# Partial outputs summed in DRAM by transfers, and seven row groups in three fp32r passes

## The chip, the cores and the metric

The kernel runs on one core of a Trainium2 chip. The metric is the device time of one execution in microseconds (us); lower is better. Engines are named as in the profile: PE is TensorE's matmuls, PEld its weight loads, DVE is VectorE, ACT is ScalarE, POOL is GpSimd and SP is SyncE. POOL and SP here issue transfers and do almost nothing else.

## The reference

Four batches of q, k and v, each 6080 rows by 256 channels in float32, go through an attention over channels, and its output through a feed-forward layer whose weights are given in float64:

```python
qn = q / (norm(q, axis=1) + 1e-6);  kn = k / (norm(k, axis=1) + 1e-6)
s = kn.transpose(0, 2, 1) @ qn / tau          # 256 x 256 per batch
a = softmax(s);  x = (v @ a).reshape(24320, 256)
h = x @ w_in                                   # 256 -> 2048
g = where(h > 0, h, exp(min(h, 0)) - 1)
out = g @ w_out                                # 2048 -> 256
```

The kernel multiplies `a` into `w_in` once per batch, so that each token needs only two products.

## The kernel before, in words

A float32 product is made in one of two ways. A plain fp32 matmul reads float32 operands as they are. The other way splits each operand into a rounded part `hi` (fp32r; ACT's cast) and a rest `lo` (DVE's subtraction), and adds three fp32r matmuls: hi·hi, hi·lo and lo·hi. Work whose operands are split by ACT and DVE while PE does something else takes the second way.

The span falls into three stages.

- **Start (0 to 58 us).** Batch 0's Gram matrix k^T q, its softmax, the product with the first part of `w_in`, and the first three of batch 1's row groups. A row group is 256 rows of q and k (two rows on each of 128 partitions), 512 KB.
- **First chunks (58 to 244 us).** Tokens are cut into 48 chunks of 496 or 512 columns. The first four (`M = 4`) run in 64 steps; `take(i)` writes one. A step makes `ph` (six matmuls, `h_item`) for one 128-row slice of the hidden layer, lets ACT and DVE turn it into `e` and split it into `g` (`elu`, `split_g`), and multiplies the `g` of three steps earlier (`LAG = 3`) into the output banks `po` (six matmuls, `out_item`). `w_in` and `w_out` arrive as float64 and are converted during these steps, so a chunk can't take all 16 slices at once: `pieces` deals the 64 steps out as 13 pieces of four or eight steps. At the end of a piece `store` empties the two `po` banks: the first piece of a chunk by an ACT copy into `half[c]` in SBUF, the later ones by a DVE addition onto `half[c]`; the last sum goes to DRAM.
- **All other chunks (244 us to the end).** Pairs of chunks with seven products for eight (`product` and `multiply_out`). A small planner with queues per engine sets their order.

In the first two stages the order on PE, DVE and ACT is the order of the code (`tc.manual_schedule`). `at(step, fn)` hangs extra work on a step, at its end: conversions of the weights (`convert`), `w_in_ready` (two matmul groups `pw`, `wp` written from them), and, for batch 1's first 12 row groups (`EARLY`), their Gram products and sums of squares. Of these 12, five (`KEPT`) are multiplied by step 0. The other seven hang at `y = 10 + 3x`: load at step y, multiply at y + 3 by `early_items` (`multiply`: four plain fp32 matmuls of 256 columns into the bank `pe`), squares at y + 4, sum of squares by a transfer at y + 5. `keep_early` copies `pe` away at step 35. DVE and ACT take their instructions strictly in the order written, as the traces show below.

Of the kernel before, what the change touches and what calls it, by code (L numbers as in the profile page):

```python
# [54 lines left out]
def channel_attention_then_elu_ffn(ctx: ExitStack, tc, q, k, vT, tau, w_in, w_out, outT):  # L55
# [8 lines left out]
    nc = tc.nc  # L64
    B, N, C = q.shape
# [14 lines left out]
    M = 4  # L80
    Q = FT // 4
    pieces = []
# [14 lines left out]
    work = ctx.enter_context(tc.tile_pool(name="work", bufs=2))  # L97
# [309 lines left out]
    def span(c):  # L407

        b, x = divmod(c, NB)
        return b, b * N + sum(sizes[:x]), sizes[x]  # L410
# [82 lines left out]
    def store(c, f, po):  # L493
        _, t0, n = span(c)
        ov = outT[:, t0 : t0 + n].rearrange("(k p) t -> p k t", p=P)
        if c < M:
            o = half[c]
        else:
            o = work.tile([P, DT, CH], F32, tag="o", bufs=1, name="o")
        for dt in range(DT):  # L500
            y, x = quarters(o[:, dt, 0:n]), quarters_of_turns(po[dt][:, 0:n])
            if c < M and (c, 0, f + 1) not in pieces:
                nc.vector.tensor_add(y, y, x)
            elif c == NCH - 1 and dt == DT - 1:

                m = n // 2
                nc.scalar.copy(y, x)
                nc.sync.dma_start(ov[:, dt, 0:m], o[:, dt, 0:m])
                nc.scalar.dma_start(ov[:, dt, m:n], o[:, dt, m:n])
                continue  # L510
            else:
                nc.scalar.copy(y, x)
            if f == FT - 1:
                nc.sync.dma_start(ov[:, dt], o[:, dt, 0:n])


    wf = {}
# [42 lines left out]
    def scratch(x, k):  # L560
        return scr[:, x * KT * CH : (x + 1) * KT * CH].rearrange("p (k n) -> p k n", k=k)

    half = {c: scratch(c, k=DT) for c in range(M)}
    sq1 = scratch(M - 1, k=2 * 2).rearrange("p (t r) c -> p t r c", t=2)

    acc = new_acc(0)
# [2 lines left out]
    state = {}  # L569

    def multiply(raw, r, gram, first, last):

        for ct in range(KT):
            nc.tensor.matmul(  # L574
                gram[ct], raw[:, 1, r, ct * P : ct * P + P], raw[:, 0, r, :], start=first[ct], stop=last[ct]
            )
# [4 lines left out]
    with tc.manual_schedule(engines={nc.sync.engine}):  # L581
# [82 lines left out]
        def early_items(n, count=[0]):  # L664
            for _ in range(n):
                x, r = divmod(count[0], 2)
                count[0] += 1
                multiply(raw1[x], r, gram1, [x == 0 and r == 0, False], [False, (x, r) == (EARLY - 1, 1)])

        spread(pn, dg)  # L670
        vraw[1] = load_v(1)
# [48 lines left out]
    def at(step, fn, free=False):  # L720
        (loose if free else side).setdefault(step, []).append(fn)
# [12 lines left out]
    at(0, lambda: early_items(2 * KEPT - 6), True)  # L734
    def keep_early():
        state["early"] = tiny.tile([P, KT, C], F32, tag="early", bufs=1, name="early")
        nc.scalar.copy(state["early"], pe)


    wis = {}  # L740
# [125 lines left out]
    def new_row():  # L866
        state.setdefault("rows", []).append(work.tile([P, 2, 2, C], F32, tag="raw", bufs=5, name="raw_1"))

    def square_row(raw, first):
        for t in range(2):  # L870
            nc.scalar.activation(state["sum"][:, t] if first else raw[:, t], raw[:, t], AF.Square)

    def add_row(raw):
        for t in range(2):
            nc.gpsimd.dma_start(state["sum"][:, t], raw[:, t], accum_op=ALU.add)
# [3 lines left out]
        state[1, "acc"] = state["sum"]  # L879
        nc.sync.dma_start(state["sum"], x)  # L880

    at(10, lambda: [new_row() for _ in range(2)])
    at(10, lambda: state.__setitem__("sum", work.tile([P, 2, 2, C], F32, tag="raw", bufs=5, name="sum")))
    at(48, move_sum)
    for x, g in enumerate((*range(KEPT, EARLY), *range(KEPT))):
        y = 10 + SPACING * x
        at(y, lambda x=x, g=g: fill_rows(state["rows"][x % 2], 1, g))
        if g >= KEPT:
            at(y + 3, lambda x=x, g=g: (raw1.append(state["rows"][x % 2]), early_items(2)), True)
        at(y + 4, lambda x=x: square_row(state["rows"][x % 2], x == 0))  # L890
        if x:
            at(y + 5 if y + 5 < 47 else max(y + 5, 49), lambda x=x: add_row(state["rows"][x % 2]))
        if g == EARLY - 1:
            at(y + 7, keep_early, True)

    def store_half():
        c = steps[-1][0]
        _, t0, n = span(c)
        nc.sync.dma_start(outT[:, t0 : t0 + n].rearrange("(k p) t -> p k t", p=P), half[c][:, :, 0:n])

    at(52, store_half)

    def load_first_w():
        state["src"] = work.tile([P, KT, CH], F32, tag="raw", bufs=5, name="wraw_0")
# [284 lines left out]
    def copy_out(c, dt):  # L1189
        _, t0, n = span(c)  # L1190
        if c < M:
            o, to = half[c][:, dt, 0:n], outT[dt * P : dt * P + P, t0 : t0 + n]
            nc.scalar.copy(quarters(o), quarters_of_turns(out_bank(c, dt)[:, 0:n]))
            task(POOL, 0.6, lambda: nc.gpsimd.dma_start(to, o, accum_op=ALU.add), when=(10, 14)[dt], level=0)
            return
        assert all(len(y) == 2 for y in operands.values())
        x = exacts[dt][:, (c - M) % 2 * CH : (c - M) % 2 * CH + CH]
        o, to = x[:, 0:n], outT[dt * P : dt * P + P, t0 : t0 + n]
        if c == NCH - 1 and dt == DT - 1:
            m = n // 2  # L1200
            y, z = o.rearrange("p (r t) -> p r t", r=2), out_bank(c, dt)[:, 0:n].rearrange("p (q r s) -> p r s q", r=2, s=2)
            y = y.rearrange("p r (s q) -> p r s q", s=2)
            nc.vector.tensor_copy(y[:, 0], z[:, 0])
            nc.scalar.copy(y[:, 1], z[:, 1])
# [539 lines left out]
```

## Time and profile before

| what | value |
|---|---|
| median of 3 runs | 2066.98 us (2065.93 to 2067.82) |
| span of the profiled execution | 2065.1 us (the page gives no other time of it) |
| PE busy | 2056.3 us, 9965 matmuls |
| DVE busy | 1592.6 us |
| ACT busy | 1431.0 us |
| granted TensorE clock | 1.000 |
| PE busy in the stage of the change, 64 to 246 us | 181.60 of 182.00 us |

The span is 1.9 us below the median of the runs; that much lies around the first and last instruction or is spread between runs. A matmul's row gives its duration with the pipeline's tail (378 ns for 512 columns); what it costs in a row of matmuls is the distance between two starts (0.216 us). The same holds for ACT and DVE, where a row overlaps its successor by about 0.09 us.

### The profile page before, as it was taken

The page shows a single profiled execution, that of the slowest core. Times are in us where ns is not written, and L with a number is a line of the kernel's source. Part 1 is how long each engine was busy: PE and PEld are TensorE (multiplying, and loading weights), DVE is VectorE, ACT ScalarE, POOL GpSimd, SP SyncE. Part 2 cuts the span into 40 slices and gives each one's busy share as a digit, 9 for nine tenths or more (in the row PEclk, how much of TensorE's full clock was granted, in tenths as well). Part 3 has the DMA queues.
Part 4 walks back from the last instruction along what each step waited for, and adds up shares of the span by engine and source line. Part 5 has one row for each costly group of instructions (what it writes and reads, how often), then busy time and mean ns, then how long its engine had stood idle before and what let it go on. Part 6 is the DMA issues. An engine that isn't in the chain of part 4 may idle for free.

```text
span 2065.1 us, 30149 instructions
## 1 busy us (share of the span) xinstructions
PE 2056.3 (100%) x9965; PEld 1824.2 (88%) x9965; DVE 1592.6 (77%) x2521; ACT 1431.0 (69%) x2423; POOL 624.8 (30%) x1083
## 2 busy tenths in 40 slices
PE   9999999999999999999999999999999999999999
PEld 8888888899888888889998888888998888888998
DVE  6978887877788777777788777777778877777775
ACT  6878767667666776776766767667776666666675
POOL 0011134442222444443223344443322222222221
PEclk9999999999999999999999999999999999999999
DMA  9457677895576989986457699897645643553533
GB/s 352 136 157 211 185 216 223 231 268 153 177 221 184 288 233 277 258 218 207 152 178 234 173 284 256 234 282 209 185 158 192 198 159 107 169 162 107 164 125 118
DMA packets 213195, 415.21 MB, mean 201 GB/s; under 512 B 23216, under 2 KB 68912, under 8 KB 210992
## 3 DMA queue, kind: packets, MB, share of 16 engines
q0 software_dynamic: 154448, 294.78, 50.6%
q1 hardware_dynamic: 58448, 118.39, 17.6%
q8 instruction: 78, 1.28, 0.3%
q14 instruction: 77, 0.63, 0.1%
q10 hardware_dynamic: 144, 0.13, 0.0%
HBM read 145.03 MB, written 30.15 MB: 85 GB/s over the span
## 4 chain that ended last, share of the span: by engine, by line
PE 97%; DVE 1%; ACT 1%; DMA 1%; issue 0%; SPq 0%; POOL 0%; DVEq 0%; POOLq 0%
PE bank_b L1164 16%; PE po L1176 14%; PE po L1175 14%; PE po L1174 14%; PE bank_e L1164 11%; PE bank_a L1164 11%; PE gram L225 4%; PE gram L574 2%; PE ph L446 1%; PE ph L448 1%; PE ph L447 1%; PE po L488 1%; PE po L490 1%; PE po L486 1%; PE pe L574 1%; PE pw L818 1%
## 5 line engine op out<-in xcount | busy, mean ns | idle before, releaser
L1176 PE MATMUL po<-g,wo 128*128 128x512 f32 (+1 forms) x1416 | 535.0, 378 | 0.0
L1175 PE MATMUL po<-t,wo 128*128 128x512 f32 (+1 forms) x968 | 366.1, 378 | 0.0
L1174 PE MATMUL po<-t,wo 128*128 128x512 f32 (+1 forms) x968 | 365.1, 377 | 0.0
L1638 DVE TENSOR_TENSOR bank_e<-bank_b,p 128x512 f32<-128x512 f32 (+1 forms) x176 | 122.0, 693 | 277.2 <-PE bank_b L1164 268.1
L1176 PEld LDWEIGHTS po<-g,wo 128*128 128x128 f32 x1416 | 267.6, 189 | 34.5
L1628 ACT COPY bank_b<-bank_a 128x512 f32<-128x512 f32 (+1 forms) x176 | 99.5, 565 | 269.9 <-PE bank_a L1164 262.4
L1242 ACT ACTIVATE other<-other 128x512 f32<-128x512 f32 (+1 forms) x396 | 248.0, 626 | 12.6
L1259 POOL DMA_DIRECT2D t<-other x242 | 128.7, 532 | 413.2 <-DVE other L1245 249.2
L1259 POOL DMA_DIRECT2D t<-held x242 | 128.8, 532 | 294.9 <-DVE held L1245 117.2
L1174 PEld LDWEIGHTS po<-t,wo 128*128 128x128 f32 x968 | 183.0, 189 | 23.4
L1175 PEld LDWEIGHTS po<-t,wo 128*128 128x128 f32 x968 | 183.1, 189 | 22.6
L1242 ACT ACTIVATE held<-held 128x512 f32<-128x512 f32 (+1 forms) x308 | 193.2, 627 | 9.8
L225 PE MATMUL gram<-qk 128*128 128x256 f32 x720 | 196.3, 273 | 0.0
L1164 PE MATMUL bank_b<-t,s 128*128 128x512 f32 (+1 forms) x576 | 188.9, 378 | 1.6 <-DVE p L1655 1.6
L1259 POOL DMA_DIRECT2D g<-other x154 | 82.0, 532 | 334.1 <-DVE other L1245 191.8
L1175 PE MATMUL po<-g,wo 128*128 128x512 f32 (+1 forms) x448 | 169.8, 379 | 0.0
L1174 PE MATMUL po<-g,wo 128*128 128x512 f32 (+1 forms) x448 | 169.1, 377 | 0.0
L1266 DVE TENSOR_TENSOR g<-held,t 128x512 fp32r<-128x512 f32 (+1 forms) x242 | 162.3, 678 | 4.5 <-DMA t<-held 4.2
L1266 DVE TENSOR_TENSOR g<-other,t 128x512 fp32r<-128x512 f32 (+1 forms) x242 | 162.7, 680 | 0.5 <-DMA t<-other 0.5
L1241 ACT ACTIVATE other<-bank_a 128x512 f32<-128x512 f32 (+1 forms) x132 | 78.1, 592 | 116.6 <-PE bank_a L1164 114.6
L1164 PE MATMUL bank_b<-g,s 128*128 128x512 f32 (+1 forms) x432 | 147.0, 377 | 0.0
L225 PEld LDWEIGHTS gram<-qk 128*128 128x128 f32 x720 | 137.7, 191 | 4.6
(288 smaller groups left out, 4912.5 us busy)
## 6 DMA issues: line engine op xcount, KB each, us to landing
t<-held POOLq DMA_DIRECT2D x154, 256.0 KB, 3.4
t<-other POOLq DMA_DIRECT2D x154, 256.0 KB, 2.6
acc<-raw POOLq DMA_DIRECT2D x118, 256.0 KB, 5.3
g<-other POOLq DMA_DIRECT2D x98, 256.0 KB, 2.3
t<-held POOLq DMA_DIRECT2D x88, 248.0 KB, 2.3
t<-other POOLq DMA_DIRECT2D x88, 248.0 KB, 2.2
raw<-in_q_dram SPq DMA_DIRECT2D x76, 256.0 KB, 3.7
raw<-in_k_dram SPq DMA_DIRECT2D x76, 256.0 KB, 4.2
```

What stands on the lines that cost most here:

```text
L225: yield nc.tensor.matmul(gram[:, ct, :], hl[:, x, 1, r, cs], in_turns(hl[:, y, 0, r, :]), start=(first and ct == 0 and r == 0 and k == 0), ...
L574: nc.tensor.matmul(gram[ct], raw[:, 1, r, ct * P : ct * P + P], raw[:, 0, r, :], start=first[ct], stop=last[ct])
L1164: nc.tensor.matmul(bank[:, 0:n], w[:, x], y, start=(begin and k == 0), stop=(k == 2), skip_group_check=True)
L1174: yield nc.tensor.matmul(o, wo[:, f, 0, ds], hi, start=begin, stop=False)
L1175: yield nc.tensor.matmul(o, wo[:, f, 1, ds], hi, start=False, stop=False)
L1176: yield nc.tensor.matmul(o, wo[:, f, 0, ds], lo, start=False, stop=end)
L1241: nc.scalar.activation(e, h, AF.Relu, scale=-1.0)
L1242: nc.scalar.activation(e, e, AF.Exp, scale=-1.0)
L1259: nc.gpsimd.dma_start(hi, e)
L1266: nc.vector.tensor_sub(lo, e, hi.bitcast(F32))
L1628: nc.scalar.copy(vb, va)
L1638: nc.vector.tensor_add(ve, vb, vp)
```

## The change

Two things are changed, both in the second stage.

1. `store` no longer adds on DVE. Every piece's two banks are copied by ACT into one of two buffers in turn; the first piece of a chunk is stored to DRAM by SP, the later ones are added onto DRAM by a POOL transfer (`accum_op=ALU.add`). The final copy from the last bank (`copy_out`) takes the next buffer in turn. `half` shrinks from four tiles to two.
2. The seven row groups that hang on the steps take three fp32r passes. They are loaded into the two scratch tiles that came free. ACT makes `early_hi` at step y + 2, DVE makes `early_lo` at step y + 3, and PE multiplies at step y + 4 (`split_items`: twelve fp32r matmuls of 256 columns instead of four fp32 ones). The five groups before them stay in fp32, but read q's columns in the order that the fp32r ones use.

```diff
     def store(c, f, po):
-        if c < M:
-            o = half[c]
+        state["stored"] = state.get("stored", 0) + 1
+        o = half[state["stored"] % 2]
+        for dt in range(DT):
+            nc.scalar.copy(quarters(o[:, dt, 0:n]), quarters_of_turns(po[dt][:, 0:n]))
+        if (c, 0, f + 1) in pieces:
+            nc.sync.dma_start(ov, o[:, :, 0:n])
         else:
-            o = work.tile([P, DT, CH], F32, tag="o", bufs=1, name="o")
-        for dt in range(DT):
-            y, x = quarters(o[:, dt, 0:n]), quarters_of_turns(po[dt][:, 0:n])
-            if c < M and (c, 0, f + 1) not in pieces:
-                nc.vector.tensor_add(y, y, x)
...
+            nc.gpsimd.dma_start(ov, o[:, :, 0:n], accum_op=ALU.add)
...
-    half = {c: scratch(c, k=DT) for c in range(M)}
+    half = [scratch(x, k=DT) for x in range(2)]
...
+        def split_items(g):
+            hl = state["split"]
+            for r in range(2):
+                for ct in range(KT):
+                    for x, y in ((0, 0), (0, 1), (1, 0)):
+                        nc.tensor.matmul(
+                            gram1[ct],
+                            hl[x][:, 1, r, ct * P : ct * P + P],
+                            in_turns(hl[y][:, 0, r, :]),
...
+    def early_hi(raw):
+        if "split" not in state:
+            state["split"] = split_rooms(F32R, ("early_hi", "early_lo"))
+        nc.scalar.copy(state["split"][0], raw)
+
+    def early_lo(raw):
+        hi, lo = state["split"]
+        nc.vector.tensor_sub(lo, raw, hi.bitcast(F32))
...
     for x, g in enumerate((*range(KEPT, EARLY), *range(KEPT))):
-        y = 10 + SPACING * x
-        at(y, lambda x=x, g=g: fill_rows(state["rows"][x % 2], 1, g))
+        y, raw = 10 + SPACING * x, early_rows[x % 2]
+        at(y, lambda raw=raw, g=g: fill_rows(raw, 1, g))
         if g >= KEPT:
-            at(y + 3, lambda x=x, g=g: (raw1.append(state["rows"][x % 2]), early_items(2)), True)
-        at(y + 4, lambda x=x: square_row(state["rows"][x % 2], x == 0))
+            at(y + 2, lambda raw=raw: early_hi(raw))
+            at(y + 3, lambda raw=raw: early_lo(raw))
+            at(y + 4, lambda g=g: split_items(g), True)
+        at(y + 4, lambda raw=raw, x=x: square_row(raw, x == 0))
...
-    at(52, store_half)
```

The order on the engines moves at the first of the seven groups like this (steps 13 and 14; `cv` is a piece of `w_out` under conversion, `wp` of the product of attention and `w_in`, `e<-e,ph` is the last operation of `elu`, `g<-e,g` the rest of `split_g`). DVE before, from step 13's `e` to step 14's:

```order
L459 SCALAR_TENSOR_TENSOR e<-e,ph 128x512
L115 TENSOR_TENSOR g<-e,g 128x512
L129 TENSOR_SCALAR cv<-cv 128x1024
L131 TENSOR_SCALAR cv<-cv 128x1024
L404 SCALAR_TENSOR_TENSOR wp_380<-pw,sums,wp_380 128x512
L459 SCALAR_TENSOR_TENSOR e<-e,ph 128x512
```

DVE now, the same stretch:

```order
L459 SCALAR_TENSOR_TENSOR e<-e,ph 128x512
L115 TENSOR_TENSOR g<-e,g 128x512
L129 TENSOR_SCALAR cv<-cv 128x1024
L131 TENSOR_SCALAR cv<-cv 128x1024
L404 SCALAR_TENSOR_TENSOR wp_380<-pw,sums,wp_380 128x512
L904 TENSOR_TENSOR early_lo<-scr,early_hi 128x1024
L459 SCALAR_TENSOR_TENSOR e<-e,ph 128x512
```

`early_lo` stands behind everything else that DVE does for step 13.

PE now, where step 14's output matmuls end and its `pw` begins; before, this place held no Gram matmuls (they stood one step earlier):

```order
L490 MATMUL po_1_731<-g,wo 128x512
L672 MATMUL pe<-early_hi 128x256
L672 MATMUL pe<-early_lo,early_hi 128x256
L672 MATMUL pe<-early_hi,early_lo 128x256
L672 MATMUL pe<-early_hi 128x256
L672 MATMUL pe<-early_lo,early_hi 128x256
```

The second matmul of a group already reads `early_lo`, and all of the following steps stand behind it on PE.

ACT now, at the end of step 12 (before, the `CAST` of `early_hi` isn't there):

```order
L114 CAST g<-e 128x512
L127 ACTIVATE cv<-wo_1_378 128x1024
L900 CAST early_hi<-scr 128x1024
L457 ACTIVATE e<-ph 128x512
L458 ACTIVATE e<-e 128x512
```

`early_hi` stands between step 12's conversion and step 13's first ACT operation.

More of the change, by code (lines that the diff above doesn't have):

```diff
@@ L495, in store @@
         ov = outT[:, t0 : t0 + n].rearrange("(k p) t -> p k t", p=P)
-        if c < M:
-            o = half[c]
-        else:
-            o = work.tile([P, DT, CH], F32, tag="o", bufs=1, name="o")
-        for dt in range(DT):
-            y, x = quarters(o[:, dt, 0:n]), quarters_of_turns(po[dt][:, 0:n])
-            if c < M and (c, 0, f + 1) not in pieces:
[L503 to L514, printed above, removed]
+        state["stored"] = state.get("stored", 0) + 1
[4 more added lines that the diff above has]
+            nc.sync.dma_start(ov, o[:, :, 0:n])
+        else:
+            nc.gpsimd.dma_start(ov, o[:, :, 0:n], accum_op=ALU.add)
     wf = {}
@@ L667, in early_items @@
                 count[0] += 1
-                multiply(raw1[x], r, gram1, [x == 0 and r == 0, False], [False, (x, r) == (EARLY - 1, 1)])
+                for ct in range(KT):
+                    nc.tensor.matmul(
+                        gram1[ct],
+                        raw1[x][:, 1, r, ct * P : ct * P + P],
+                        in_turns(raw1[x][:, 0, r, :]),
+                        start=(x == 0 and r == 0 and ct == 0),
+                        stop=False,
+                        skip_group_check=True,
+                    )
+        def split_items(g):
+            hl = state["split"]
+            for r in range(2):
+                for ct in range(KT):
+                    for x, y in ((0, 0), (0, 1), (1, 0)):
+                        nc.tensor.matmul(
+                            gram1[ct],
+                            hl[x][:, 1, r, ct * P : ct * P + P],
+                            in_turns(hl[y][:, 0, r, :]),
+                            start=False,
+                            stop=((g, r, ct, x) == (EARLY - 1, 1, KT - 1, 1)),
+                            skip_group_check=True,
+                        )
         spread(pn, dg)
@@ L736, in keep_early @@
         state["early"] = tiny.tile([P, KT, C], F32, tag="early", bufs=1, name="early")
-        nc.scalar.copy(state["early"], pe)
+        for ct in range(KT):
+            nc.scalar.copy(halves(state["early"][:, ct]), halves_of_turns(pe[:, ct]))
     wis = {}
@@ L880, in move_sum, with split_rooms @@
         nc.sync.dma_start(state["sum"], x)
-    at(10, lambda: [new_row() for _ in range(2)])
+    def split_rooms(dtype, names):
+        return [work.tile([P, 2, 2, C], dtype, tag="raw", bufs=5, name=name) for name in names]
+    def early_hi(raw):
[5 more added lines that the diff above has]
+        nc.vector.tensor_sub(lo, raw, hi.bitcast(F32))
+    early_rows = [scratch(x, k=2 * 2).rearrange("p (t r) c -> p t r c", t=2) for x in (2, 3)]
+    at(10 + SPACING * (EARLY - KEPT) + 3, lambda: [new_row() for _ in range(2)])
     at(10, lambda: state.__setitem__("sum", work.tile([P, 2, 2, C], F32, tag="raw", bufs=5, name="sum")))
@@ L885, in channel_attention_then_elu_ffn @@
     for x, g in enumerate((*range(KEPT, EARLY), *range(KEPT))):
-        y = 10 + SPACING * x
-        at(y, lambda x=x, g=g: fill_rows(state["rows"][x % 2], 1, g))
+        y, raw = 10 + SPACING * x, early_rows[x % 2]
+        at(y, lambda raw=raw, g=g: fill_rows(raw, 1, g))
         if g >= KEPT:
-            at(y + 3, lambda x=x, g=g: (raw1.append(state["rows"][x % 2]), early_items(2)), True)
-        at(y + 4, lambda x=x: square_row(state["rows"][x % 2], x == 0))
+            at(y + 2, lambda raw=raw: early_hi(raw))
+            at(y + 3, lambda raw=raw: early_lo(raw))
+            at(y + 4, lambda g=g: split_items(g), True)
+        at(y + 4, lambda raw=raw, x=x: square_row(raw, x == 0))
         if x:
-            at(y + 5 if y + 5 < 47 else max(y + 5, 49), lambda x=x: add_row(state["rows"][x % 2]))
+            at(y + 5 if y + 5 < 47 else max(y + 5, 49), lambda raw=raw: add_row(raw))
         if g == EARLY - 1:
             at(y + 7, keep_early, True)
[L896 to L899, printed above, removed]
-    at(52, store_half)
     def load_first_w():
@@ L1191, in copy_out @@
         if c < M:
-            o, to = half[c][:, dt, 0:n], outT[dt * P : dt * P + P, t0 : t0 + n]
+            o, to = half[(state["stored"] + 1) % 2][:, dt, 0:n], outT[dt * P : dt * P + P, t0 : t0 + n]
             nc.scalar.copy(quarters(o), quarters_of_turns(out_bank(c, dt)[:, 0:n]))
```

## The prediction

> **What bounds the kernel now.** I read the page first: the span, PE's share, and the chain that ended last. Then came the busy times of the stage that is changed, and what PE waits for in it.
>
> ```profile
> span 2065.1 us, 30149 instructions
> PE 2056.3 (100%) x9965; PEld 1824.2 (88%) x9965; DVE 1592.6 (77%) x2521; ACT 1431.0 (69%) x2423; POOL 624.8 (30%) x1083
> ...
> PE 97%; DVE 1%; ACT 1%; DMA 1%; issue 0%; SPq 0%; POOL 0%; DVEq 0%; POOLq 0%
> ...
> 64.00:246.00 182.00, 181.60 (x839) 157.91 (x837) 153.94 (x227) 148.32 (x256) 23.95 (x28) 1.00 0.57 159
> ...
> PE po L488 <- DVE wo L549: 0.2, 1, 0.2
> ```
>
> PE is the bound, and in the changed stage it is as good as full: 181.60 of 182.00 us, with one wait of 0.2 us. DVE (153.94) and ACT (148.32) are less full, but not by much. So two things count: the matmul time that is taken from PE, and every wait that is put in front of PE where none was. Work taken from DVE is worth nothing by itself, since PE does not wait for it here.
>
> **The change part by part.** *The matmuls.* These are PE's rows around the first of the seven groups (steps 13 and 14), and two neighbours of the fp32r Gram form from a later batch:
>
> ```profile
> 94.72 1.89 PE L574 MATMUL pe<-raw 128*128 128x256 f32 x8
> ...
> 97.74 0.38 PE L446 MATMUL ph<-scr_r,wp 128*128 128x512 f32 x1
> ...
> 98.82 0.38 PE L448 MATMUL ph<-scr_r,wp 128*128 128x512 f32 x1
> ...
> 100.11 0.38 PE L490 MATMUL po<-g,wo 128*128 128x512 f32 x1
> ...
> 317.12 0.27 PE L225 MATMUL gram<-qk 128*128 128x256 f32 x1
> 317.23 0.38 PE L1175 MATMUL po<-g,wo 128*128 128x512 f32 x1
> ```
>
> One group is four fp32 matmuls, shown as eight records; 1.89 less a tail of 0.16 (0.38 less the 0.216 between starts) is 1.73 us. Now it is twelve fp32r matmuls of 256 columns; such a matmul moves the next start by 0.11 us (317.12 to 317.23), so 1.32 us. That is 0.41 us less a group, **2.9 us less** for seven. Above 0.11 the price is bounded by 0.21, if a weight load (0.19 us in its row below) could not run under so short a matmul; I take 0.11, the form's own row. The five groups before stay fp32 at the same count; that they read their columns in another order I cost at nothing, within 0.2 us.
>
> *The wait that is added.* A group now needs `early_lo`, which DVE makes at the end of the step before. These are ACT's and DVE's rows there, and the means of the conversion pieces that stand ahead of it:
>
> ```profile
> 90.31 1.04 ACT L114 CAST wi<-wf 128x1024 fp32r<-128x1024 f32 x1
> 91.26 0.59 ACT L457 ACTIVATE e<-ph 128x512 f32<-128x512 f32 x1
> ...
> 94.39 0.58 ACT L457 ACTIVATE e<-ph 128x512 f32<-128x512 f32 x1
> 95.00 0.63 ACT L458 ACTIVATE e<-e 128x512 f32<-128x512 f32 x1
> ...
> 99.23 0.60 ACT L457 ACTIVATE e<-ph 128x512 f32<-128x512 f32 x1 [0.61 <-PE ph L448]
> ```
>
> ```profile
> 91.47 1.22 DVE L115 TENSOR_TENSOR wi<-wf,wi 128x1024 fp32r<-128x1024 f32 x1
> ...
> 95.66 0.69 DVE L459 SCALAR_TENSOR_TENSOR e<-e,ph 128x512 f32<-128x512 f32 x1 [1.77 <-ACT e L458]
> 96.27 0.68 DVE L115 TENSOR_TENSOR g<-e,g 128x512 fp32r<-128x512 f32 x1
> 96.87 0.69 DVE L129 TENSOR_SCALAR cv<-cv 128x1024 f32<-128x1024 f32 x1
> 97.59 0.69 DVE L131 TENSOR_SCALAR cv<-cv 128x1024 uint32<-128x1024 uint32 x1
> 98.66 0.75 DVE L404 SCALAR_TENSOR_TENSOR wp<-pw,sums,wp 128x512 fp32r<-128x512 f32 x1 [0.38 <-ACT wp L403]
> 100.53 0.69 DVE L459 SCALAR_TENSOR_TENSOR e<-e,ph 128x512 f32<-128x512 f32 x1 [1.11 <-ACT e L458]
> ```
>
> The first group by itself. `early_hi` is a 1024-wide cast, 0.95 us of ACT (90.31 to 91.26), put where ACT has no gap: step 13's first ACT operation moves from 94.39 to 95.34, and with it DVE's `e` from 95.66 to 96.61. Behind it follow, at the distances of the rows, `g` 97.22, L129 97.82, L131 98.54, L404 99.15 (0.61 on; `pw` now ends 1.73 earlier, so ACT no longer delays it), and `early_lo` 99.81. That is an operation like the L115 of 1.22 us, so it ends at 101.03. PE meanwhile: step 13's output matmuls end at 94.72; `pw` (six at 0.216) to 96.02; step 14's hidden and output matmuls 2.59 us (97.74 to 100.33) to 98.61; hi·hi to 98.72. Then it waits for `early_lo`: **2.4 us** with 0.05 for the signal.
>
> The other six by the same count. From the last hidden matmul (98.82) ACT begins 0.41 later (99.23), DVE's `e` 1.30 after that (100.53); `g` 0.60 and a gap of 0.60, then 1.22 for `early_lo`: 102.95. PE comes to the lo matmul at 100.33 + 2.59 + 0.11 = 103.03. So a step with nothing else has 0.08 us to spare, and what stands between `g` and `early_lo` becomes the wait. By the order these are L143 at step 16, L129 and L131 at 19, L141 at 22, nothing at 25, L133 at 28 and L141 at 31:
>
> ```profile
> L133 DVE SCALAR_TENSOR_TENSOR cv<-wo,cv 128x1024 uint32<-128x1024 uint32 x3 | 4.5, 1492 | 0.0
> L141 DVE SCALAR_TENSOR_TENSOR cv_s<-wi,cv_s 128x1024 f32<-128x1024 uint32 x3 | 4.5, 1487 | 0.0
> L141 DVE SCALAR_TENSOR_TENSOR cv_s<-wo,cv_s 128x1024 f32<-128x1024 uint32 x3 | 4.2, 1397 | 0.0
> L143 DVE TENSOR_TENSOR cv<-cv,cv_s 128x1024 f32<-128x1024 f32 x3 | 3.7, 1218 | 0.0
> ...
> L457 ACT ACTIVATE e<-ph 128x512 f32<-128x512 f32 x63 | 37.2, 591 | 26.9 <-PE ph L448 26.9
> ...
> 114.79 0.38 PE L448 MATMUL ph<-scr_r,wp 128*128 128x512 f32 x1
> ...
> 116.67 0.57 ACT L457 ACTIVATE e<-ph 128x512 f32<-128x512 f32 x1
> ```
>
> Less 0.09 of overlap each: 1.13 + 1.32 + 1.40 + 0 + 1.40 + 1.31 = 6.6, less six times 0.08 is 6.1 us. That is the lower end, with 0.6 for the first group if `early_hi` cost nothing there: 6.7 in all. The upper end lets `early_hi` push every step by its full 0.95 (5.7) and keeps 2.4 for the first: 14.2; lateness that ACT has anyway comes on top. I take the middle that the rows give. ACT waits for PE 26.9 us ahead of 63 such operations, 0.43 each, so `early_hi` pushes by 0.52: 6.1 + 3.1 + 2.4 = 11.6. At step 19 ACT is already late: 116.67 against 114.79 + 0.41, by 1.47 us; I count half of that, since the waits before let ACT catch up, and as much again for DVE's backlog and ACT's store copies, so 1.2: **12.8 us of waits**.
>
> A wait also costs PE a restart. The longest wait of before, in the third stage, shows it, with the clock's first matmuls of the span beside it:
>
> ```profile
> 268.30 0.38 PE L1176 MATMUL po<-g,wo 128*128 128x512 f32 x1
> 270.08 0.92 PE L1164 MATMUL bank_b<-t,s 128*128 128x512 f32 x3 [1.41 <-DVE p L1655]
> 270.83 0.38 PE L1174 MATMUL po<-g,wo 128*128 128x512 f32 x1
> ...
> 268.14 0.68 DVE L1266 TENSOR_TENSOR g<-other,g 128x512 fp32r<-128x512 f32 x1
> ...
> 3.80 2.05 PE L574 MATMUL gram<-ragged 128*128 128x256 f32 x4
> 6.50 1.91 PE L574 MATMUL gram<-room 128*128 128x256 f32 x8
> ```
>
> After the gap three matmuls take 0.75 us instead of 0.65: 0.1 a wait, **0.7 us** for seven. The same rows show that PE does not go past a matmul that waits: L1174, whose `g` DVE had finished by 268.82, starts at 270.83. Were PE able to pass it, the seven waits would cost little and the sum would be the 2.9 us of gain. The Trainium skill ("TensorE: Matmul & The Clock Gate", "Part 2: What happens when you issue a matmul") says that only weight loads are pulled ahead and that matmuls stay in program order; by that rule the waits count in full, and the trace agrees with the 270.83 above.
>
> *The stores.* DVE loses 16 additions, ACT gains 16 copies:
>
> ```profile
> L503 DVE TENSOR_TENSOR scr<-scr,po 128x512 f32<-128x512 f32 x16 | 10.3, 686 | 0.0
> L512 ACT COPY scr<-po 128x512 f32<-128x512 f32 x8 | 4.3, 582 | 0.0
> ...
> acc<-raw POOLq DMA_DIRECT2D x118, 256.0 KB, 5.3
> ...
> raw<-in_q_dram SPq DMA_DIRECT2D x76, 256.0 KB, 3.7
> ```
>
> 16 × 0.60 us off DVE and 16 × 0.49 onto ACT, with seven `early_hi` 14.5 us in all, against 182.00 − 148.32 = 33.7 us that ACT has free. PE gains nothing from DVE's freed time; it can lose where ACT is full for a while, 0 to 1 us, and I take 0. The eight transfers that add onto DRAM stand on POOL's queue behind ACT's copies. Their nearest row is the adding transfer of half the size, 5.3 us to landing; a buffer is used again two pieces later, at least eight steps of 2.59 us, so even 10.6 us are hidden. On that queue `s<-x` for the third stage's second quarter now stands behind the last three of them, while DVE's work just ahead of that stage gets shorter. What that does to the stage's first waits I bound by the 1.41 us of the longest, gained or lost once more, and take 0. SP's queue gets four small stores earlier and loses later ones. The loads (3.7 us) have two steps, 5.2 us, before `early_hi`; late ones would stop ACT, which the range has to carry.
>
> **Sum.** −2.9 + 12.8 + 0.7 = +10.6 us on the profiled span of 2065.1, so 2075.7. The median of the runs lies 1.9 us above that span: **2077.6 us**.
>
> **The rivals.**
> - *The gain arrives.* DVE and ACT run so far ahead that `early_lo` is there: 2067.0 − 2.9 = 2064.1 us. For it: DVE is idle a sixth of the stage. Against it: both engines begin a step's work only when its hidden matmuls end, so free time before that cannot be used; it decides where the chain above is shorter than PE's 4.2 us from 98.82 to 103.03. With the third stage's wait of 1.41 us gone too, it would be 2062.7.
> - *The short matmuls cost 0.21.* Twelve weight loads in a row do not hide: 7 × 12 × 0.1 = 8.4 us more, 2086. Against it: in the row at 317.23 the next load hid under one short matmul; for it: there the neighbours are long.
> - *The clock.* At the span's start a record of the same fp32 matmul costs 0.51 us (2.05 for four), later 0.24 (1.91 for eight). If each of the seven waits brought that back for as long as it lasted at the start, at most to 5.85 us (3.80 + 2.05), half of that would be lost: 2.9 us each, 20 in all, 2098. Against it: the gap of 1.77 us before 270.08 was followed by near full rate. The Trainium skill (same page, "Part 1: The HAM clock gate") gives 3.4 us of idling as the window after which the clock halves; the waits above stay under it, so by that rule this does not happen.
>
> **How the numbers follow.** Waits as worked out: 0.73, with its own range from 2065.1 + 1.9 − 2.9 + 6.7 + 0.7 − 1.5 = 2070 to 2083 (14.2 and 2.4 more for lateness and late loads, with 1.5 of the seam, the 1.41 rounded). The gain arrives: 0.12 at 2064, and 0.04 at 2062.7 with the later wait gone. Short matmuls dear: 0.07. Clock: 0.04. The range 2069 to 2087 leaves out the second and the last, 0.2. A measurement of this kernel tells about 0.2%, 4.1 us: slower by more is the first case nearly whole with the last two, 0.82; faster by more only the one at 2062.7, 0.04; the rest 0.14.
>
> **What would show it.** Seven PE waits on DVE's `early_lo` between 95 and 175 us, 1 to 3 us each, at the second matmul of a group; PE busy lower by about 3 us and idle higher by about 13; no PE wait on the stores; the third stage the same as before but 10 us later. The prediction is wrong if these waits are absent or short, if ACT stops at `early_hi` for a load, or if a group's twelve matmuls take more than 1.4 us of PE without a wait.

## The result and the profile after

The changed kernel takes 2083.18 us in the median of 5 runs (2082.73 to 2083.79), against 2066.98 us for the kernel before in the same comparison: a ratio of 1.0081 (95% interval 1.0070 to 1.0091), so it is slower by 0.8%. The profiled execution took 2083.44 us, with a span of 2081.7 us.

The page of the changed kernel, the same parts that were shown of before:

```profile
span 2081.7 us, 30227 instructions
PE 2060.9 (99%) x9993; PEld 1825.8 (88%) x9993; DVE 1592.6 (77%) x2512; ACT 1444.9 (69%) x2447; POOL 635.3 (31%) x1091
...
PE 91%; ACT 3%; DVE 3%; issue 2%; DMA 1%; POOL 0%; ACTq 0%; POOLq 0%; DVEq 0%
```

The span grew by 16.6 us. PE was to become less busy and became busier, by 4.6 us. The chain that ended last was PE for 97% and is PE for 91% now: ACT and DVE have come into it, which means that PE stands and waits for them. The 4.6 us of busy time are, within 0.1, half rate and turned reads, which are read below, and the restart and the tail of a matmul at each of seven waits, less what the shorter matmuls save.

What PE waits for (total us, times, longest), whole span of the changed kernel:

```profile
PE pe L672 <- DVE early_lo L904: 12.1, 7, 2.6
PE bank_b L1184 <- DVE p L1675: 1.6, 2, 1.4
```

These are the seven waits of the forecast, at the line of `split_items`, and this list has no other new one in the stage. The wait at the third stage's beginning is as before. Weight loads have a list of their own (PEld), and it has two new waits at steps 44 to 46, small ones; the experiment e8 comes back to them:

```profile
PEld po L490 <- DVE g L115: 0.5, 1, 0.5
PEld po L486 <- ACT g L114: 0.3, 1, 0.3
```

The stage by windows of 15 us (length, PE busy and its matmuls, granted clock, DMA share, GB/s):

```profile
90.00:105.00 15.00, 12.66 (x60) 0.91 0.35 141
105.00:120.00 15.00, 12.96 (x65) 0.97 0.37 113
120.00:135.00 15.00, 12.38 (x56) 0.89 0.52 112
```

PE idles for 2.0 to 2.6 us in each of them. The clock column shows something that the kernel before did not have in this stage, where it was 1.00 throughout: 0.91, 0.97 and 0.89 around the first and the third group.

### The profile page after: what moved, and what is told of

Same layout as the page of the kernel before. It is cut to its first block, busy times and chain, and to the rows that moved or that the text cites. A ratio compares the mean times of both kernels' runs of the same rounds, so it can differ in the third digit from the quotient of the medians.

```text
span 2081.7 us, 30227 instructions
## 1 busy us (share of the span) xinstructions
PE 2060.9 (99%) x9993; PEld 1825.8 (88%) x9993; DVE 1592.6 (77%) x2512; ACT 1444.9 (69%) x2447; POOL 635.3 (31%) x1091
## 3 DMA queue, kind: packets, MB, share of 16 engines
q0 software_dynamic: 156624, 298.98, 51.5%
## 4 chain that ended last, share of the span: by engine, by line
PE 91%; ACT 3%; DVE 3%; issue 2%; DMA 1%; POOL 0%; ACTq 0%; POOLq 0%; DVEq 0%
PE bank_b L1184 16%; PE po L1195 14%; PE po L1196 14%; PE po L1194 14%; PE bank_e L1184 11%; PE bank_a L1184 11%; PE gram L225 4%; PE gram L563 2%; ACT e L457 1%; PE pe L658 1%; PE pe L672 1%; PE pw L830 0%; PE pw L829 0%; PE pw L828 0%; DVE g L115 0%
```

## The waits and the clock, row by row

PE's rows of the changed kernel at the first three groups (start, duration; in brackets the idle time before and what released it):

```profile
100.03 0.27 PE L672 MATMUL pe<-early_hi 128*128 128x256 f32 x1
102.64 0.58 PE L672 MATMUL pe<-early_lo,early_hi 128*128 128x256 f32 x1 [2.34 <-DVE early_lo L904]
103.01 0.42 PE L672 MATMUL pe<-early_hi,early_lo 128*128 128x256 f32 x1
...
104.93 0.42 PE L672 MATMUL pe<-early_hi,early_lo 128*128 128x256 f32 x1
105.14 0.63 PE L396 MATMUL pw<-wi,aT_split 128*128 128x512 f32 x1
105.57 0.53 PE L397 MATMUL pw<-wi,aT_split 128*128 128x512 f32 x1
105.94 0.38 PE L398 MATMUL pw<-wi,aT_split 128*128 128x512 f32 x1
...
114.57 0.27 PE L672 MATMUL pe<-early_hi 128*128 128x256 f32 x1
116.88 0.38 PE L672 MATMUL pe<-early_lo,early_hi 128*128 128x256 f32 x1 [2.04 <-DVE early_lo L904]
117.09 0.28 PE L672 MATMUL pe<-early_hi,early_lo 128*128 128x256 f32 x1
117.20 0.28 PE L672 MATMUL pe<-early_hi 128*128 128x256 f32 x1
...
125.98 0.27 PE L672 MATMUL pe<-early_hi 128*128 128x256 f32 x1
128.88 0.38 PE L672 MATMUL pe<-early_lo,early_hi 128*128 128x256 f32 x1 [2.62 <-DVE early_lo L904]
...
129.76 0.42 PE L672 MATMUL pe<-early_hi,early_lo 128*128 128x256 f32 x1
...
130.61 0.63 PE L446 MATMUL ph<-scr_r,wp 128*128 128x512 f32 x1
...
133.17 0.38 PE L486 MATMUL po<-g,wo 128*128 128x512 f32 x1
```

Read the distance between starts. The second group is as forecast: one wait, then 0.11 us from matmul to matmul. After the first wait the distance is 0.21 until 104.93 and 0.43 for the `pw` behind, so everything takes twice its time; from 105.94 on it is normal. After the third wait PE works at full rate for 0.9 us, and only from 129.76 on, in the middle of the group, at half rate, until 133.17. That second stretch is 3.41 us long, and none of its matmuls waits for anything.

DVE's rows at the third group show what PE waits for: `early_lo` stands behind both conversion pieces and ends at 128.82, and PE goes on at 128.88.

```profile
126.28 0.69 DVE L129 TENSOR_SCALAR wf<-wf 128x1024 f32<-128x1024 f32 x1
127.00 0.69 DVE L131 TENSOR_SCALAR wf<-wf 128x1024 uint32<-128x1024 uint32 x1
127.60 1.22 DVE L904 TENSOR_TENSOR early_lo<-scr,early_hi 128x1024 fp32r<-128x1024 f32 x1
```

From the seven pairs of rows (first matmul to second, less the 0.11 that it would take) the waits sum to 2.50 + 2.20 + 2.79 + 1.40 + 0.94 + 1.55 + 1.85 = 13.2 us. The second matmul then takes 0.21 (116.88 to 117.09), so a restart is 0.1, in seven groups another 0.8: 14.0 us. The matmuls themselves are twelve at 0.11, 1.33 us a group, so 2.8 us less than the 7 × 1.73 of before. Half rate costs 1.57 us within the first and third group, 0.37 in the `pw` behind the first and 1.26 in the six `ph` behind the third: 3.2 us.

One more term shows before the stage. PE's rows of the five groups that stayed fp32, at 49 us, in the changed kernel:

```profile
48.97 3.44 PE L658 MATMUL pe<-scr 128*128 128x256 f32 x12
52.24 0.49 PE L357 MATMUL pt<-ident,a 128*128 128x128 f32 x3
```

and the same twelve in the kernel before:

```profile
49.47 2.75 PE L574 MATMUL pe<-scr 128*128 128x256 f32 x12
52.06 0.67 PE L357 MATMUL pt<-ident,a 128*128 128x128 f32 x3
```

Twelve records took 2.59 us and take 3.27 now: 0.273 apiece for 0.216. Only the order in which they read q's columns was changed. For the forty records of five groups that is 2.2 us, by the starts of all their rows.

The sum is 14.0 − 2.8 + 3.2 + 2.2 = 16.6 us. The rows above stand 0.5 us earlier than those of before at this point, so the steps should start 16.1 us later behind the groups; from step 48 on they start 16.05 us later. That this agrees so closely is partly luck: up to step 10 the steps have lost 1.9 us and not 2.2, and steps 35 to 48 add 0.2 that is not in the sum (0.5 less at step 35, where a pause of before is gone, and 0.7 more at the two waits of the weight loads). The last 0.5 us to the 16.6 of the span come after that.

## The experiments

The theory at that point: PE loses by the waits for `early_lo`, by half rate after the longer ones, and by the turned reads of the fp32 groups; the stores cost nothing. The rival: the stores, with eight more transfers on POOL's queue, carry part of the loss by themselves.

**e1, the stores alone.** All twelve groups are multiplied in fp32 at y + 3, in plain column order, as before.

```diff
-            at(y + 2, lambda raw=raw: early_hi(raw))
-            at(y + 3, lambda raw=raw: early_lo(raw))
-            at(y + 4, lambda g=g: split_items(g), True)
+            at(y + 3, lambda raw=raw: (raw1.append(raw), early_items(2)), True)
...
-                        in_turns(raw1[x][:, 0, r, :]),
+                        raw1[x][:, 0, r, :],
```

> Only the stores by transfer; the seven row groups stay four plain fp32 matmuls at step y + 3, straight from the scratch tiles, and the five earlier groups read in plain order. Theory: the stores cost and bring nothing, since PE waited for no store before and ACT and POOL have the room: 2066.0 to 2068.5 us, no PE wait above 0.5 us between 64 and 246 us. Rival: the additions in DRAM or ACT's copies cost part of the 16 us: 2070 us or more, with PE waits on ACT or on g in that stage.

Measured: 2074.29 us in the median, ratio 1.0033 (1.0021 to 1.0046), and widely spread: 2068.97 to 2077.37 in six runs, where the kernel before stays within 3.7 us in 33. The expectation missed that. The profiled execution was the fastest of the six and shows no wait in the stage longer than 0.2 us, so it could not say what the others lost; e11 below does.

**e2, one more step for `early_lo`.** The changed kernel with the multiplications at y + 5.

```diff
-            at(y + 4, lambda g=g: split_items(g), True)
+            at(y + 5, lambda g=g: split_items(g), True)
```

> The changed kernel with split_items one step later (y + 5 instead of y + 4), nothing else. Theory: the 13.2 us of waits on early_lo and the 3.2 us of slow clock behind them vanish: 2083.2 - 16.4 = 2066.8 us (2065.5 to 2069), clock 1.000, no PE wait on early_lo. Rival: the wait only changes its place, since early_hi of the next group now needs the tile that PE still reads: ACT stops there and PE waits for g, 2072 us or more.

Measured: 2076.71 us (2073.32 to 2078.55), ratio 1.0046 (1.0034 to 1.0058). The waits for `early_lo` are gone as expected (0.2 us is left), but a gain of 16 was expected and 6.5 came. PE's and ACT's longest waits in the stage, then SP's:

```profile
PE ph L446 <- DVE e L459: 5.3, 1, 5.3
ACT early_hi L900 <- DMA scr<-in_k_dram: 6.5, 1, 6.5
```

```profile
SPq L159 <- DMA sum<-scr: 74.5, 18, 11.9
```

At one place ACT stood 6.5 us at `early_hi` for raw rows that had not landed, DVE's `e` came late behind it, and PE stood 5.3 us. SP must not write the tile before the transfer that adds up its squares has read it (L159 waits for `sum<-scr`, up to 11.9 us). That wait is as long in the kernel before, so it is not new by itself:

```profile
SPq L159 <- DMA sum<-raw: 74.2, 16, 13.0
```

New is that ACT, and behind it PE, stand when such a load comes later than usual. So a second wait stands behind the first one, in the loads; e11 shows what makes one late.

**e3, the waits filled.** The changed kernel with matmuls of a zero weight (256 columns, 4 to 18 a group) put where PE waits, so that the waits stay and PE does not stand idle.

```diff
+                        for _ in range(fill):
+                            nc.tensor.matmul(
+                                gram1[ct], zeros, in_turns(hl[0][:, 0, r, :]), start=False, stop=False, skip_group_check=True
+                            )
```

> The changed kernel, with 16, 14, 18, 8, 4, 9 and 12 matmuls of zero weights put behind the first matmul of the seven groups, so that PE works through most of each wait (0.11 us each) and idles 1.2 us at most. Theory: the waits stay (PE still needs early_lo at the same time) and the clock no longer falls: 2083.2 - 3.2 = 2080.0 us (2079 to 2081), clock 1.000, all L672-type matmuls 0.11 us apart. Rival: the slow matmuls behind the waits are not from idling: 2083 us or more with the 0.21 us distances still there.

Measured: 2080.4 us (2079.69 to 2081.01), as expected, 2.8 us below the changed kernel, although the changed kernel has fewer matmuls to do. The first and third of the windows above, and the wait that is left:

```profile
90.00:105.00 15.00, 14.45 (x81) 1.00 0.35 141
120.00:135.00 15.00, 14.38 (x82) 1.00 0.44 107
```

```profile
PE pe L678 <- DVE early_lo L915: 3.3, 7, 0.6
```

The clock is 1.00 in both, and over the whole span. Half rate after the waits is a cost of its own, of about 3 us, and it comes from PE standing idle, not from the twelve short matmuls.

**e4, plain column order.** The changed kernel, with q's columns read in plain order by both kinds of groups.

```diff
-                        in_turns(raw1[x][:, 0, r, :]),
+                        raw1[x][:, 0, r, :],
...
-                            in_turns(hl[y][:, 0, r, :]),
+                            hl[y][:, 0, r, :],
```

> The changed kernel with all reads of q's columns for the bank pe in plain order, the five fp32 groups and the seven fp32r ones, and the copy of pe in plain order. Theory: the five groups' records go back from 0.27 to 0.216 us apart, 2.3 us less, and the fp32r matmuls keep 0.11: 2080.9 us (2080 to 2082). Rival: an fp32r matmul needs the turned order for its rate and takes 0.2 us in plain order: seven groups 7.5 us longer, 2088 us.

Measured: 2080.66 us (2079.87 to 2082.04), 2.5 us below the changed kernel, with 11.8 us of waits for `early_lo`. The twelve fp32 records are back at 2.59 us:

```profile
48.70 2.75 PE L658 MATMUL pe<-scr 128*128 128x256 f32 x12
51.29 0.77 PE L357 MATMUL pt<-ident,a 128*128 128x128 f32 x4
```

These rows, and not the time, show the price of the turned reads. The time met its expectation, but it holds other terms too: this profile has one stretch at half rate (126.7 to 130.1 us) where the changed kernel has two, about 1.5 us less, and its fp32r matmuls take 0.119 us apiece for 0.111, which is 0.7 more.

**e5, e2 without the sums.** As e2, but the transfers that add up batch 1's squares are not issued (their sums are left out beyond the first group).

> As the kernel with the split multiplications one step later (2076.7 us), but without the eleven transfers that add up batch 1's squares (their sums are left out beyond the first group). Theory: what was left of its loss is late loads: a load waits for the summing transfer of the group before to have read its scratch tile, ACT stops at `early_hi` for the load, and PE for ACT's `e` (5.3 us at one place of its profile). Without the transfers the loads start in time, no PE wait on `e` or `early_lo` above 0.5 us is left in the stage, and the time is 2066.8 us (2065.5 to 2068.5): 2066.3, less 2.9 for the fp32r matmuls, plus 2.3 for the five fp32 groups' turned reads and about 1 for a restart or two. Rival: the loss comes from ACT's copies or the DRAM additions themselves: the time stays at 2073 or above.

Measured: 2066.77 us (2065.71 to 2067.90), ratio 1.0001 (0.9992 to 1.0009). The forecast was 2066.8. No PE wait is left in the stage, and ACT no longer waits for a load. So what e2 still lost goes with the sums. Leaving them out takes away their transfers as well as the wait of the loads for them; the rows of e2 and e11 are what names the loads.

**e6, `early_lo` first.** The changed kernel with `early_lo` ahead of the step's conversion on DVE, the multiplications still at y + 4.

```diff
-            at(y + 3, lambda raw=raw: early_lo(raw))
+            loose.setdefault(y + 3, []).insert(0, lambda raw=raw: early_lo(raw))
```

> The changed kernel, but `early_lo` is put ahead of the step's conversion on DVE (right behind `g`) and not behind it; the multiplications stay at y + 4. Theory: what stands between `g` and `early_lo` is the wait, so the waits fall from 13.2 us by the 6.6 us of conversion pieces to some 6.6, no wait is above 2.1 us, and the stretches at half clock (3.2 us) go: 2083.2 - 6.6 - 3.2 = 2073.4 us (2071 to 2076). Rival: the pieces were not what was waited for (ACT is late, or the load): the waits stay at 10 us or more, and the time is 2079 or above.

Measured: 2071.34 us (2070.34 to 2073.03), ratio 1.0023 (1.0015 to 1.0032).

```profile
PE pe L672 <- DVE early_lo L904: 3.9, 5, 1.5
```

The waits fell by 8.2 us and the granted clock of the span is 1.000. So it was the conversion pieces that stood between `g` and `early_lo`, as the forecast named them; the waits fell by 1.6 us more than the pieces themselves, and the time came out 2.1 us below the expectation.

**e7, `early_hi` later.** `early_hi` and `early_lo` both at y + 3, the multiplications at y + 5, plain column order: the load gets one step more.

```diff
-            at(y + 2, lambda raw=raw: early_hi(raw))
+            loose.setdefault(y + 3, []).insert(0, lambda raw=raw: early_hi(raw))
...
-            at(y + 4, lambda g=g: split_items(g), True)
+            at(y + 5, lambda g=g: split_items(g), True)
```

> Everything found so far put together: `early_hi` a step later and `early_lo` in the step of `early_hi` (y + 3), the multiplications at y + 5, so that the load has one step more and DVE nearly a whole step; q's columns in plain order everywhere, so the five fp32 groups cost what they did. Theory: 2066.3 - 2.9 = 2063.4 us, with up to 3 us for loads that are still late now and then: 2063 to 2067. Rival: a group's scratch tile is held a step longer by nothing, but the load still starts only when the summing transfer is done, at 6 to 11 us: ACT stops all the same, and the time is 2070 or above.

Measured: 2065.4 us (2064.89 to 2070.08), ratio 0.9996 (0.9987 to 1.0005): as fast as before and not faster. The profiled execution was the longest of the eleven, and a late load is what it shows:

```profile
ACT early_hi L899 <- DMA scr<-in_k_dram: 6.1, 1, 6.1
```

**e8, e1 without the sums.** (The sums of batch 1's squares are left out as in e5.)

> The kernel with the new stores alone (2074.3 us in the median, 2069 to 2077), without the eleven transfers that add up batch 1's squares (their sums are left out beyond the first group). Theory: the stores cost PE time because their DRAM additions slow the summing transfers, these free the scratch tiles late, and the loads and what reads them come late: without the sums 2066 to 2068 us, with a spread below 2 us. Rival: the ACT copies or the DRAM additions cost by themselves, whatever else moves: 2070 to 2077 as before, and as widely spread.

Measured: 2068.31 us (2067.72 to 2071.02), ratio 1.0009 (1.0000 to 1.0018). That is a little above the expectation, and so is the spread of 3.3 us. Six of the eight us that the stores cost in e1, and most of the spread, went away with the sums, which the stores themselves don't touch. The other 2 us are not in the groups: from step 0 to step 44 the steps keep their distance to those of before to 0.01 us. They lie in three places.

At steps 44 to 46 the kernel loses 0.66 us. These are the two waits of weight loads that were shown for the changed kernel (here 0.26 and 0.52 us): the store's two copies take ACT 1.07 us at the end of a piece, its next `e` comes later, and PE's weight loads wait for `g`. Every version with the new stores loses 0.66 to 0.69 us at this place. Another 1.2 us lie behind the last matmul, where ACT issues the last transfer; before, then here:

```profile
2062.07 0.37 ACTq L1206 DMA_DIRECT2D out_dram<-exact  x1
2062.72 1.57 ACTq L1223 DMA_DIRECT2D out_dram<-exact  x1
```

The four profiles with the stores alone (e1, e8, e9, e11) have this row at 1.57 to 1.60 us, all others at 0.37 or 0.38; why is open. The third stage loses some 0.8 us in small pieces, and this execution had started its steps 0.8 us early.

**e9, stores without adding.** As e1, but the eight POOL transfers write without `accum_op` (the earlier partial sums of the first four chunks are left out of the output).

> The kernel with the new stores alone (2074.3 us in the median, 2069 to 2077), but its eight POOL transfers write to DRAM without adding (the earlier pieces' partial sums of the first four chunks are left out of the output); the transfers that add up batch 1's squares are back. Theory: it is the adding, which moves each of its 512 KB twice, that slows the sums and so the loads: 2066 to 2069 us with a spread below 2. Rival: two more streams on the queues are enough, or the copies: 2072 us or more, widely spread.

Measured: 2071.91 us (2070.04 to 2073.59), ratio 1.0025 (1.0015 to 1.0036). It lies between the two expectations. The transfers cost 5.5 us without adding, so the adding is not what most of the loss needs. That adding costs the other 2.4 us is not shown: e1's six runs spread over 8.4 us, and the two kernels' times overlap. What became smaller is the spread, 3.6 us in eight runs. The queue's bytes are counted alike with and without adding (298.98 MB on both pages), so these pages don't show either that adding moves every byte twice.

**e11, e1 once more, for an ordinary execution.** The kernel is that of e1.

> The kernel with the new stores alone once more, for a profile of an ordinary execution (its first profile fell on the fastest one, 2069.0 us; the others were up to 2077.4). Theory: at 2072 to 2078 us the profile shows PE waiting 4 to 9 us in all in steps 10 to 46, for one or two late loads of raw rows (their DMA named directly by PE's fp32 Gram matmuls, or by ACT's squares and behind them `e`). Rival: the loss is spread over ACT copies at the pieces' ends, or lies in the third stage.

Measured: 2076.21 us. PE's one long wait in the stage:

```profile
150.62 3.75 PE L658 MATMUL pe<-scr 128*128 128x256 f32 x8 [5.45 <-DMA scr<-in_k_dram]
```

One group of raw k rows was late. PE stood 5.5 us, and the eight records behind took 3.75 us, twice the 1.89 of the prediction's row: again half rate. The steps up to 28 stand 0.2 us behind those of before, those from 30 on 7.8. SP issued this load at 144.04 here and at 140.37 in the fastest execution, the profile of e1. It left 3.7 us later (the steps stand 1.4 us later in this execution), and PE could use it 6.6 us after that. Between 129 and 142 us the sums of the group that held the tile shared the queues with a store of a finished piece, a load of weights and, from 141.76 on, a transfer that adds onto DRAM. These two sums took this long from issue to landing, in the kernel before and here:

```profile
DMA to landing us min/median/max: 3.9/4.2/4.6
DMA to landing us min/median/max: 8.7/10.2/11.7
```

The kernel before has the load of weights at this place too, but not the store. The two sums were issued at 131.82 and 132.36, so the first had landed when the adding transfer was issued and the second had 2.3 us left; and without adding, in e9, they take 7.7 and 10.3 us. At this place it is thus not the adding that slows the sums, as e8 and e9 expected; the store of the finished piece is what is new beside them, though no run moves it alone. The adding transfer ran beside the late load. Whether a load comes in time is decided by a few us there, which fits e1's wide spread.

**e10, the squares added by DVE.** As e7, but the sums up to step 46 are DVE additions at y + 5 and no transfers.

```diff
-            at(y + 5 if y + 5 < 47 else max(y + 5, 49), lambda raw=raw: add_row(raw))
+            if y + 5 < 47:
+                at(y + 5, lambda raw=raw: nc.vector.tensor_add(state["sum"], state["sum"], raw))
+            else:
+                at(max(y + 5, 49), lambda raw=raw: add_row(raw))
```

> As the kernel with `early_hi` later, the multiplications at y + 5 and plain column order (2065.4 us, up to 2070.1), but the squares of the groups up to step 46 are added by DVE at y + 5 (1.22 us each, of the time that its 16 store additions took before) and not by transfers. Theory: a load then waits for nothing that takes 6 to 11 us, no PE wait is left among steps 10 to 35, and the time is 2064.0 us (2063 to 2065.5) with a spread below 2. Rival: the additions delay DVE's `e` and `g` and PE waits for these: 2067 or more.

Measured: 2066.26 us (2064.78 to 2068.11), ratio 0.9998 (0.9989 to 1.0007), above the expected range and no faster than before. Within the stage it does what was hoped: no PE wait among steps 10 to 42, and from step 0 to step 36 PE gains 2.6 us on the kernel before. Of these, 2.1 are the groups (1.43 us each for 1.73; in plain column order an fp32r matmul takes 0.119 us for the 0.111 of the turned order), and 0.5 is a pause at step 35 that the kernel before has and this one has not. Steps 44 to 48 take 0.66 back, and the beginning of the third stage another 2.6. PE's row there, and the stretch behind it as a window (length, PE busy and its matmuls, granted clock, DMA share, GB/s):

```profile
267.56 0.92 PE L1186 MATMUL bank_b<-t,s 128*128 128x512 f32 x3 [1.98 <-DVE p L1677]
```

```profile
268.52:271.93 3.41, 3.41 (x9) 0.50 0.54 169
```

The wait for `p` that was 1.41 us before is 1.98 here, and half rate follows, for 3.41 us, which costs 1.7. PE came early into the third stage and had to wait for it.

## Why the prediction was right, and where it was not

The time was forecast as 2077.6 us with a range of 2069 to 2087, and slower with 0.82. The side and the mechanism were right; the size was 5.6 us short.

- *The matmuls, −2.9.* Right: −2.8 in the rows, 1.33 us a group for the forecast's 1.32. (The row of a weight load that the forecast points at is not among its lines; the page of before has them at 189 ns.) The rival of short matmuls at 0.21 fell: the second group shows 0.11 from its third matmul on. Where 0.21 does show, at the first group, the clock is the reason, since the 512-column matmuls behind it double too and e3 removes it.
- *The waits, 12.8, and restarts, 0.7.* Right in place, count and size: seven, for `early_lo`, at the second matmul of a group, 14.0 us with their restarts against 13.5. The pieces that stand there are those that were named for each group. The first wait was forecast at 2.4 and took 2.5. The other six come, by the forecast's count, to 1.6, 3.0, 1.8, 0.4, 1.8 and 1.8 us, and measured 2.2, 2.8, 1.4, 0.9, 1.6 and 1.9: up to 0.6 off, both ways, so that the sum is this near is in part luck. The forecast's addition has a slip too: half of 1.47 and as much again are 1.5 and not 1.2, which makes 13.1. That PE does not go past a matmul that waits holds in all seven. e6 confirms what the waits are made of.
- *The clock, given 0.04.* This rival came true in part, and it is one of the two mis-sized terms: 3.2 us in place of 0 (and of the rival's 20). By the forecast's own sign of being wrong, a group of more than 1.4 us without its wait, the first group (2.6) and the third (1.8) are wrong; the others take 1.44 with their restart, which the forecast counts by itself. Its argument against itself was the wait before 270.08, which full rate had followed; the 1.77 us that it gives are about the distance from the start before, and the idle time in the row is 1.41. Here waits of 2.34 and 2.62 us were followed by half rate. The two stretches at half rate are 3.41 us long each and begin 27.31 us apart, which is eight times 3.41. So the trace can be cut into windows of 3.41 us that end where a stretch begins. The windows around the first three waits:

```profile
99.04:102.45 3.41, 1.26 (x7) 1.00 0.00 0
102.45:105.86 3.41, 3.22 (x13) 0.50 0.42 159
112.69:116.10 3.41, 2.15 (x11) 1.00 0.05 19
116.10:119.51 3.41, 2.63 (x18) 1.00 0.04 8
126.34:129.75 3.41, 0.87 (x7) 1.00 0.00 0
129.75:133.16 3.41, 3.41 (x12) 0.50 0.62 112
```

  The windows ahead of the two slow ones are idle for 2.15 and 2.54 us. The second wait, of 2.04 us, is cut into 1.26 and 0.78 by the end of a window, and the clock stays. The trace of e4 has a sharper case: a wait of 2.22 us, cut into 1.29 and 0.93, and full rate after it:

```profile
95.99:99.40 3.41, 2.12 (x11) 1.00 0.00 0
99.40:102.81 3.41, 2.48 (x16) 1.00 0.41 159
102.81:106.22 3.41, 3.41 (x17) 1.00 0.47 125
```

  Shorter waits that lie in one window were followed by half rate: 1.96 us in e9, 1.98 in e10, and in e7 two waits that leave 1.25 and 0.88 us in the same window. Laid out like this, from the clock's first rise to the last work, the traces of all versions agree: a window with 1.98 us of idling or more is followed by half rate, and one with 1.71 or less is not. Between these there are three, 1.91 (e4) and 1.96 (e9) with half rate behind them and 1.95 (e4) without. So it is the idling of a window that counts and not the length of a wait, and the limit lies between 1.7 and 2.0 us of the 3.41. No run moved a wait across the end of a window on purpose. The page that was cited in the forecast, "TensorE: Matmul & The Clock Gate" of the Trainium skill ("Part 1: The HAM clock gate"), has the clock fall after an idle window of about 3.4 us. Here page and measurement differ, since windows that were only partly idle were enough, and the measurement decides. Another sentence of that section says that the window is 3413 ns long and runs freely. The stretches of 3.41 us, eight of their lengths apart, agree with it.
- *The five kept groups, "at nothing, within 0.2".* The other mis-sized term: 2.2 us, since an fp32 matmul that reads its columns in turned order takes 0.273 us a record in place of 0.216; in e4 the rows go back with the order. The seven groups in fp32r read in the same turned order at 0.11 and lose nothing by it.
- *The stores, 0.* Nearly right for the changed kernel: 0.7 us, at the two waits of weight loads behind ACT's copies, within the 0 to 1 that the forecast allowed; but for a reason that was not given: ACT waits for no load of raw rows there as long as PE is late anyhow. What failed is the ranking of it: "late ones would stop ACT" stood in the range alone, while with the waits for `early_lo` gone (e2) or never made (e1) leaving out the sums is worth 9.9 us (e5 against e2) and 6.0 (e8 against e1). The forecast counted the transfers' landing against the next use of the store's buffer; what is slower beside the new stores is the sums, which free the tiles of the loads. That the gain could be had by taking the waits away, as the rivals of 2064.1 us supposed, needs the loads freed as well; e7 and e10, which try it, come to 2065.4 and 2066.3.
- *The seam, 0.* Right: the waits there are the same, and 0.5 us was lost after step 48.

The 5.6 us that the forecast is short are thus 3.2 of the clock and 2.2 of the turned reads; the 0.5 of the waits and restarts and the 0.5 behind step 48 are about balanced by this execution's start, 0.5 us early, and by the 1.5 us, not 1.9, from its span to the median. No version that was run is faster than the kernel before by more than the measurement tells.

Still open: why the last transfer's issue takes 1.2 us longer with the stores alone, and how the loss of e1 divides between the stores of finished pieces, DRAM's adding and the mere number of transfers.

## What to carry to other kernels

Before PE is given work that needs another engine's result, count what stands ahead of that result on its engine since the last event that it depends on: here that count, from rows of the profile before, gave the sum of the waits to within 4% and the single ones to within 0.6 us, and a step more of distance removed them. Then ask what was hidden behind the wait, because a transfer that "lands in time" shares its queues with others, and a tile is free for its next load only when the slowest reader is done. And a change of the order in which a matmul reads its operand is a change of its cost until a row shows that it is not.

## What was not expected of the hardware

- Half rate came in stretches of 3.41 us on a grid of that length, each behind a window that was idle for 1.9 us or more; none followed 1.7 us or less. A wait of 2.22 us that a window's end cut in two was not followed by it (e4), one of 1.96 us was (e9), and it began up to 1.5 us after PE had gone on (e4: from 125.21 on at full rate, at half from 126.71). The dearest wait of the changed kernel, 2.79 us, cost 4.5 with what followed (0.40 in its group, 1.26 behind it).
- An fp32 matmul of 256 columns with a turned read of its moving operand: 0.273 us a record in place of 0.216. The fp32r form goes the other way: 0.111 turned, 0.119 plain.
- Twelve fp32r matmuls of 256 columns in a row, each with a weight load of its own (0.19 us long by itself): 0.11 us each.
- Two transfers of 256 KB that add up squares in SBUF took 3.9 and 4.6 us to land before, and 8.7 and 11.7 with a store of 512 KB just ahead of them (e11); that the store is the cause is not shown. With the new stores alone a kernel's runs spread over 8.4 us (e1) in place of 3.7, and over 3.3 without these sums (e8).
